# Sparse attention and two mixing layers on one core: GpSimd's two-operand instructions issued in pieces of at most 300 elements

## The chip, the cores and the metric

The kernel runs on one core of a Trainium2 chip. A core has five engines that work side by side, each through its own queue of instructions in order: TensorE (PE in the profile; its weight loads are PEld), VectorE (DVE), ScalarE (ACT), GpSimd (POOL) and SyncE (SP), which here only issues DMAs. They share SBUF, the on-chip memory of 128 partitions; matrix products land in PSUM, which GpSimd doesn't read. The metric is the device time of one execution in microseconds (us).

## What is computed

The reference has three parts. Attention over 4 batches, 8 heads, 576 positions and 64 columns a head keeps the 32 largest scores of each row; two mixing layers follow, the first with a rotation by an angle, the second with a normalised gate.

```python
scores = scale * np.matmul(q, k.transpose(0, 1, 3, 2))
kth = np.partition(scores, -top_k, axis=-1)[..., -top_k:-top_k + 1]
scores = np.where(scores >= kth, scores, -1000000000.0)
attn = np.exp(scores - np.max(scores, axis=-1, keepdims=True))
attn = attn / (np.sum(attn, axis=-1, keepdims=True) + 1e-09)
...
theta = x @ w_theta
y = w_tok_r @ (x * np.cos(theta)) + w_tok_i @ (x * np.sin(theta))
u = x + y
x = u + np.maximum(u @ w_ch, 0.0)
...
h = np.maximum(x @ w_in, 0.0)
u, v = h[..., :d_ff // 2], h[..., d_ff // 2:]
v_s = w_spatial @ normalised(v) + b_spatial
out = (u * v_s) @ w_out
```

The six weights arrive as float64. Products that need near-float32 accuracy are made of three matrix products on operands that are split into a high and a low part; the low part is the difference of a value and its rounded copy, and such differences are much of what GpSimd does.

## The kernel before

Attention runs over 144 tiles (4 batches, 4 pairs of heads, 9 tiles of 128 query rows), two tiles to a group, so 72 groups. `scores` multiplies a tile's queries with the keys and ScalarE copies the 576 scores of each row to `x` (L433). `topk` works on a group's two tiles on VectorE: L448 and L449 halve the row twice by pairwise maximum and minimum (two instructions on 2x288 elements, two on 2x144, listed as 576 and 288), then MAX8 and MATCH_REPLACE8 take out the 32 largest in four rounds. L465 compares four elements a row to `flags`, and L471 makes the threshold `cf`. `weigh` lets ScalarE compute a sign against the threshold (L480) and the exponential (L481); GpSimd multiplies the two into `sg`, 576 elements a tile (L482). `transpose` turns `sg` on TensorE (L491), ScalarE copies the result to `ptb` (L492), and `values` multiplies by the values (L513). `normalise` divides by the row sum, on GpSimd (L544, L547).

Beside that run the conversion of the weights (`split_weights`, L143 to L194: VectorE assembles float32 from the two words of a double, GpSimd makes the high and low part), the preparation of the next heads (`prep`; GpSimd's difference is L374), and the two mixing layers of the batches that are through attention (`rotate`, `middle`, `last`), a few matrix products after each attention step. The mixing layers go through a wrapper `Urgent` that raises an instruction's priority, so the profile shows all of their elementwise work under L568.

No engine's order is written out by hand. The framework's scheduler orders the instructions by priorities and by its own model of their durations. A change in the number or size of instructions can therefore move others on every engine. The program ends with a second, exact copy of all of this that is taken only if a flag is set; it isn't taken here. GpSimd is reached under two names: `pool`, and `upool`, which is `Urgent` around it.

Of the kernel before, what the change touches and what calls it, by code (L numbers as in the profile page):

```python
# [24 lines left out]
def sparse_attention_then_moe_kernel(  # L25
# [20 lines left out]
    nc = tc.nc  # L46
# [25 lines left out]
    dram = ctx.enter_context(tc.tile_pool(name="dram", bufs=1, space=bass.MemoryType.DRAM))  # L72
    psum = ctx.enter_context(tc.tile_pool(name="psum", bufs=1, space=bass.MemoryType.PSUM))

    act, dve, pool, pe = nc.scalar, nc.vector, nc.gpsimd, nc.tensor

    def f32(ap):
        return ap.bitcast(F32)
# [237 lines left out]
    def run(exact):  # L316
# [242 lines left out]
        class Urgent:  # L559
# [5 lines left out]
            def __getattr__(self, name):  # L565
                def call(*args, **kwargs):
                    with tc.high_priority(offset=URGENT):
                        return getattr(self.engine, name)(*args, **kwargs)  # L568

                return call  # L570

        udve, uact, upool = Urgent(nc.vector), Urgent(nc.scalar), Urgent(nc.gpsimd)

        def copy_pool(out, x):
            upool.tensor_scalar(out, x, 1.0, 0.0, op0=OP.mult, op1=OP.add)
# [447 lines left out]
        advance(1e12)  # L1023

    run(False)
    flagged = nc.values_load(count[0:1, 0:1], min_val=0, max_val=128)
    with tc.If(flagged > 0):
        run(True)
# [42 lines left out]
```

## Time and profile before

| | before |
|---|---|
| time, median of 3 runs | 993.77 us (988.09 to 994.96) |
| the profiled execution's own time | 986.55 us |
| its span, first to last instruction | 984.8 us |
| TensorE busy | 854.1 us |
| VectorE busy | 837.5 us |
| ScalarE busy | 626.2 us |
| GpSimd busy | 546.2 us, 476 instructions |

Busy time counts an instruction from its recorded start to its end. An instruction on VectorE or GpSimd that has started and is held up inside still counts as busy, so for these two engines the busy time can hold waiting. Idle time is split by what ended it.

### The profile page before, as it was taken

The page shows a single profiled execution, that of the slowest core. Times are in us where ns is not written, and L with a number is a line of the kernel's source. Part 1 is how long each engine was busy: PE and PEld are TensorE (multiplying, and loading weights), DVE is VectorE, ACT ScalarE, POOL GpSimd, SP SyncE. Part 2 cuts the span into 40 slices and gives each one's busy share as a digit, 9 for nine tenths or more (in the row PEclk, how much of TensorE's full clock was granted, in tenths as well). Part 3 has the DMA queues.
Part 4 walks back from the last instruction along what each step waited for, and adds up shares of the span by engine and source line. Part 5 has one row for each costly group of instructions (what it writes and reads, how often), then busy time and mean ns, then how long its engine had stood idle before and what let it go on. Part 6 is the DMA issues. An engine that isn't in the chain of part 4 may idle for free.

```text
span 984.8 us, 17792 instructions
## 1 busy us (share of the span) xinstructions
PE 854.1 (87%) x5802; PEld 785.8 (80%) x5802; DVE 837.5 (85%) x2710; ACT 626.2 (64%) x1298; POOL 546.2 (55%) x476
## 2 busy tenths in 40 slices
PE   3656677785898999898998999799899999999997
PEld 2555666664797988897898998698889998889987
DVE  6999999899999998899999998999999951463552
ACT  5666767678767567777867777577957764350121
POOL 1686776658685854758385656375655553420030
PEclk9865676687899999999999999899999999999999
DMA  7797774647638463544461844352742645341221
GB/s 218 222 333 224 238 220 150 171 139 203 219 105 241 164 167 140 157 150 100 147 162 32 276 152 144 126 161 71 229 138 68 258 155 181 156 181 52 103 86 53
DMA packets 79393, 159.76 MB, mean 162 GB/s; under 512 B 36143, under 2 KB 40239, under 8 KB 71866
## 3 DMA queue, kind: packets, MB, share of 16 engines
q1 hardware_dynamic: 79290, 158.53, 51.0%
q8 instruction: 48, 0.79, 0.3%
q14 instruction: 55, 0.45, 0.1%
HBM read 108.63 MB, written 23.32 MB: 134 GB/s over the span
## 4 chain that ended last, share of the span: by engine, by line
DVE 46%; PE 32%; ACT 7%; DMA 7%; issue 4%; POOL 3%; SPq 1%; DVEq 0%; ACTq 0%; POOLq 0%
DVE mm L449 8%; PE ps_m L552 7%; DVE mx L458 7%; PE ps_m L553 7%; PE ps_m L554 7%; DVE mm L461 7%; DVE z L452 5%; DVE mm L448 4%; PE ps_v L513 4%; PE ps_s L429 2%; PE ps_t L491 2%; DVE F L568 2%; DMA q<-hi 2%; DVE z L448 2%; DVE cf L471 2%
## 5 line engine op out<-in xcount | busy, mean ns | idle before, releaser
L482 POOL TENSOR_TENSOR sg<-x,sg 128x576 f32<-128x576 f32 x144 | 213.0, 1495 | 150.9 <-ACT x L481 90.9
L513 PE MATMUL ps_v<-vc,ptb 128*128 128x65 f32 (+1 forms) x1280 | 176.6, 277 | 15.1 <-ACT ptb L492 15.1
L513 PEld LDWEIGHTS ps_v<-vc,ptb 128*128 128x128 f32 (+1 forms) x1280 | 167.4, 201 | 24.4 <-ACT ptb L492 18.5
L491 PE MATMUL ps_t<-ident,sg 128*128 128x128 f32 x648 | 132.0, 305 | 42.2 <-POOL sg L482 33.5
L480 ACT ACTIVATE sg<-x,cf 128x576 f32<-128x576 f32 x144 | 103.8, 769 | 56.0 <-DVE cf L471 53.2
L491 PEld LDWEIGHTS ps_t<-ident,sg 128*128 128x128 f32 x648 | 93.7, 166 | 53.9 <-POOL sg L482 39.0
L458 DVE MAX8 mx<-mm 128x8 f32<-128x160 f32 x432 | 118.9, 313 | 0.0
L433 ACT ACTIVATE x<-ps_s 128x576 f32<-128x576 f32 x144 | 92.4, 642 | 32.0 <-POOL sg L482 16.8
L429 PE MATMUL ps_s<-k,q 128*128 128x288 f32 x256 | 91.2, 367 | 24.1 <-ACT x L433 15.0
L552 PE MATMUL ps_m<-w_t,zah 128*128 128x288 f32 (+2 forms) x272 | 98.7, 363 | 11.3 <-DVE F L568 6.7
L481 ACT ACTIVATE x<-x,cf 128x576 f32<-128x576 f32 x144 | 108.0, 767 | 0.1
L492 ACT ACTIVATE ptb<-ps_t 128x640 f32<-128x640 f32 (+1 forms) x144 | 92.4, 642 | 13.2 <-PE ps_t L491 12.3
L554 PE MATMUL ps_m<-w_t,zal 128*128 128x288 f32 (+2 forms) x272 | 96.6, 355 | 0.6 <-DVE zal L568 0.4
L553 PE MATMUL ps_m<-w_t,zah 128*128 128x288 f32 (+2 forms) x272 | 96.5, 355 | 0.0
L452 DVE MAX8 z<-mm 128x8 f32<-128x312 f32 (+1 forms) x288 | 89.5, 372 | 1.9
L552 PE MATMUL ps_m<-w_t,zbh 128*128 128x288 f32 x288 | 85.9, 301 | 3.2 <-DVE F L568 1.9
L461 DVE MATCH_REPLACE8 mm<-mx,mm 128x160 f32<-128x160 f32 x288 | 87.0, 309 | 0.0
L553 PE MATMUL ps_m<-w_t,zbh 128*128 128x288 f32 x288 | 85.4, 300 | 0.6 <-DMA w_t<-d_spl 0.6
L554 PE MATMUL ps_m<-w_t,zbl 128*128 128x288 f32 x288 | 84.3, 299 | 1.0 <-POOL zbl L568 1.0
L552 PE MATMUL ps_m<-ph,w_t 128*128 128x288 f32 x256 | 76.8, 301 | 8.1 <-DMA w_t<-d_chh 4.3
L429 PEld LDWEIGHTS ps_s<-k,q 128*128 128x128 f32 x256 | 55.8, 218 | 33.1 <-ACT x L433 24.6
L449 DVE TENSOR_TENSOR mm<-x 128x576 f32<-128x576 f32 x72 | 82.2, 1141 | 0.0
(175 smaller groups left out, 2391.4 us busy)
## 6 DMA issues: line engine op xcount, KB each, us to landing
k<-hi SPq DMA_DIRECT2D x60, 144.0 KB, 2.6
kl<-raw SPq DMA_DIRECT2D x60, 144.0 KB, 3.1
vc<-in_v_dram SPq DMA_DIRECT2D x48, 128.0 KB, 2.8
w_t<-d_trh SPq DMA_DIRECT2D x4, 1152.0 KB, 5.2
w_t<-d_trl SPq DMA_DIRECT2D x4, 1152.0 KB
out_dram<-t SPq DMA_DIRECT2D x32, 144.0 KB, 2.2
raw<-in_q_dram SPq DMA_DIRECT2D x15, 288.0 KB, 3.0
q<-hi SPq DMA_DIRECT2D x30, 144.0 KB, 2.8
```

The lines of the kernel that those rows point to most:

```text
L429: pe.matmul(o, q, k[:, m], start=a == 0, stop=a == len(terms) - 1)
L449: dve.tensor_tensor(mm[:, :, mid:hi], a, b, op=OP.min)
L452: dve.max(out=z[:, i, QUARTER + 8 * k:QUARTER + 8 * k + 8], in_=mm[:, i, losers])
L458: last = dve.max(out=top[i], in_=src[i])
L461: dve.match_replace(out=mr[i], in_to_replace=top[i], in_values=src[i], imm_value=NEG)
L481: act.activation(x, x, AF.Exp, bias=cf[:, 0:1], scale=0.125)
L482: pool.tensor_tensor(sg, x, sg, op=OP.mult)
L491: pe.transpose(pt[:, c, :], x[:, lo:lo + 128], ident)
L513: pe.matmul(o, pt[:, c, q], chunks[:, c, slot], start=alone and c == 0, stop=not alone and i == 1 and c == 3)
L552: pe.matmul(out, ah, bh, start=first, stop=False)
L553: pe.matmul(out, ah, bl, start=False, stop=False)
L554: pe.matmul(out, al, bh, start=False, stop=last)
```

## The change

The name `pool` no longer stands for GpSimd itself but for an object that passes everything on to it, save `tensor_tensor`: that one is issued in k pieces along the first free dimension, where k is the number of elements a partition divided by 300 and rounded up, but no more than that dimension's length. `upool` is wrapped around the same object. Instructions with one operand (`tensor_scalar`, `memset`) stay whole, and so do those of up to 300 elements.

```diff
-    act, dve, pool, pe = nc.scalar, nc.vector, nc.gpsimd, nc.tensor
+    act, dve, pe = nc.scalar, nc.vector, nc.tensor
+
+    class Pieces:
+
+
+        def __getattr__(self, name):
+            return getattr(nc.gpsimd, name)
+
+        def tensor_tensor(self, out, a, b, op):
+            n = out.shape[1]
+            k = -(-math.prod(out.shape[1:]) // 300)
+            k = min(k, n)
+            cuts = [n * i // k for i in range(k + 1)]
+            for lo, hi in zip(cuts, cuts[1:]):
+                nc.gpsimd.tensor_tensor(out[:, lo:hi], a[:, lo:hi], b[:, lo:hi], op=op)
+
+    pool = Pieces()
...
-        udve, uact, upool = Urgent(nc.vector), Urgent(nc.scalar), Urgent(nc.gpsimd)
+        udve, uact, upool = Urgent(nc.vector), Urgent(nc.scalar), Urgent(pool)
```

All pieces stand under L89 afterwards, and the other lines of the kernel are 16 higher. A shape of three dimensions is cut in its first: the 5x2x64 of `xn` becomes 128, 256 and 256 elements. TensorE's instructions and their order in the last fifth of the program are the same; before that the scheduler has set the order anew.

GpSimd, early in the program, where the first weights are converted (`w_f`, `w_hi`) between multiplications of `sg`. Before:

```order
L194 TENSOR_TENSOR w_f<-w_f,w_hi 128x1024
L374 TENSOR_TENSOR raw<-raw,hi 128x576
L482 TENSOR_TENSOR sg<-x,sg 128x576
L193 TENSOR_SCALAR w_hi<-w_f 128x1152
L482 TENSOR_TENSOR sg<-x,sg 128x576
L194 TENSOR_TENSOR w_f<-w_f,w_hi 128x1152
```

Now, at the same place:

```order
L89 TENSOR_TENSOR w_f<-w_f,w_hi 128x256 x4
L89 TENSOR_TENSOR raw<-raw,hi 128x288 x2
L209 TENSOR_SCALAR w_hi<-w_f 128x1152
L89 TENSOR_TENSOR w_f<-w_f,w_hi 128x288 x4
L89 TENSOR_TENSOR sg<-x,sg 128x288 x6
```

Each whole has become two or four pieces, and the multiplications of `sg` that stood ahead of the 1152-element difference now stand behind its four pieces.

GpSimd in the middle of the program, where `middle` of the first batch splits its `F` (`pl`) beside attention. Before:

```order
L194 TENSOR_TENSOR w_f<-w_f 128x512
L482 TENSOR_TENSOR sg<-x,sg 128x576
L568 TENSOR_TENSOR pl<-F,ph 128x288 x7
L482 TENSOR_TENSOR sg<-x,sg 128x576
L568 TENSOR_TENSOR pl<-F,ph 128x288
L374 TENSOR_TENSOR raw<-raw,hi 128x576
```

Now:

```order
L89 TENSOR_TENSOR w_f<-w_f 128x256 x2
L89 TENSOR_TENSOR pl<-F,ph 128x288 x5
L89 TENSOR_TENSOR sg<-x,sg 128x288 x4
L89 TENSOR_TENSOR pl<-F,ph 128x288
L89 TENSOR_TENSOR raw<-raw,hi 128x288 x2
L89 TENSOR_TENSOR sg<-x,sg 128x288 x2
```

The seven `pl`, which were short enough to stay whole, stood in a row between two `sg`; now five stand ahead of both.

VectorE in the 37th turn of `topk`. Before:

```order
L448 TENSOR_TENSOR mm<-x 128x2x288
L449 TENSOR_TENSOR mm<-x 128x2x288
L465 TENSOR_TENSOR flags<-z,mx 128x4
L471 SCALAR_TENSOR_TENSOR cf<-cf,mx 128x2
L448 TENSOR_TENSOR z<-mm 128x2x144
L449 TENSOR_TENSOR mm<-mm 128x2x144
L452 MAX z<-mm 128x8 x4
```

Now:

```order
L481 TENSOR_TENSOR flags<-z,mx 128x4
L584 TENSOR_TENSOR F<-ps_m,F 128x288 x2
L487 SCALAR_TENSOR_TENSOR cf<-cf,mx 128x2
L464 TENSOR_TENSOR mm<-x 128x2x288
L465 TENSOR_TENSOR mm<-x 128x2x288
L584 TENSOR_TENSOR F<-ps_m,F 128x288
L464 TENSOR_TENSOR z<-mm 128x2x144
L465 TENSOR_TENSOR mm<-mm 128x2x144
L468 MAX z<-mm 128x8 x4
```

The six steps with two operands in SBUF still stand in one stretch; additions to `F` from PSUM, steps of the mixing layers, have moved in between them.

## Rows read from the trace of the kernel before

**Rows 1.** The page: span, and the busiest engines.

```profile
span 984.8 us, 17792 instructions
...
PE 854.1 (87%) x5802; PEld 785.8 (80%) x5802; DVE 837.5 (85%) x2710; ACT 626.2 (64%) x1298; POOL 546.2 (55%) x476
```

**Rows 2.** Busy time by stretch; each engine: us (instructions).

```profile
core 0: us, PE busy (x) PEld busy (x) DVE busy (x) ACT busy (x) POOL busy (x), PEclk, DMA share, GB/s
0.00:200.00 200.00, 130.78 (x627) 111.02 (x628) 187.60 (x589) 133.05 (x263) 125.42 (x116) 0.71 0.74 222
200.00:770.00 570.00, 518.64 (x3755) 483.27 (x3754) 549.99 (x1827) 416.08 (x873) 359.44 (x299) 0.96 0.49 150
770.00:984.00 214.00, 204.64 (x1424) 191.47 (x1423) 99.87 (x296) 77.09 (x162) 61.30 (x61) 0.99 0.38 141
```

**Rows 3.** Groups by line and shape, VectorE: busy us, mean ns, idle before.

```profile
L449 DVE TENSOR_TENSOR mm<-x 128x576 f32<-128x576 f32 x72 | 82.2, 1141 | 0.0
L448 DVE TENSOR_TENSOR mm<-x 128x576 f32<-128x576 f32 x72 | 69.0, 958 | 11.4 <-ACT x L433 11.1
...
L449 DVE TENSOR_TENSOR mm<-mm 128x288 f32<-128x288 f32 x72 | 41.2, 572 | 1.3
...
L448 DVE TENSOR_TENSOR z<-mm 128x288 f32<-128x288 f32 x72 | 35.7, 495 | 0.0
...
L465 DVE TENSOR_TENSOR flags<-z,mx 128x4 uint8<-128x4 f32 x72 | 29.1, 404 | 1.3
L471 DVE SCALAR_TENSOR_TENSOR cf<-cf,mx 128x2 f32<-128x2 f32 x72 | 28.9, 402 | 1.0 <-ACT cf L470 0.6
```

**Rows 4.** Time line of VectorE, an undisturbed turn: start us, us taken.

```profile
166.89 0.16 DVE L465 TENSOR_TENSOR flags<-z,mx 128x4 uint8<-128x4 f32 x1
...
167.57 0.17 DVE L471 SCALAR_TENSOR_TENSOR cf<-cf,mx 128x2 f32<-128x2 f32 x1
167.64 0.46 DVE L448 TENSOR_TENSOR z<-mm 128x288 f32<-128x288 f32 x1
...
169.10 1.24 DVE L452 MAX8 z<-mm 128x8 f32<-128x312 f32 x4
...
174.16 0.75 DVE L448 TENSOR_TENSOR mm<-x 128x576 f32<-128x576 f32 x1
```

**Rows 5.** Time line of GpSimd near 512 us.

```profile
511.94 2.03 POOL L374 TENSOR_TENSOR raw<-raw,hi 128x576 fp32r<-128x576 f32 x1
513.93 1.32 POOL L568 TENSOR_TENSOR pl<-F,ph 128x288 fp32r<-128x288 f32 x1
```

**Rows 6.** Time line of VectorE near 512 us.

```profile
512.60 1.99 DVE L449 TENSOR_TENSOR mm<-x 128x576 f32<-128x576 f32 x1
514.51 0.77 DVE L471 SCALAR_TENSOR_TENSOR cf<-cf,mx 128x2 f32<-128x2 f32 x1
515.20 0.45 DVE L568 TENSOR_TENSOR F<-ps_m,F 128x288 f32<-128x288 f32 x1
```

**Rows 7.** Time line of GpSimd near 328 us.

```profile
327.26 0.79 POOL L568 TENSOR_TENSOR pl<-F,ph 128x288 fp32r<-128x288 f32 x1
328.02 1.41 POOL L374 TENSOR_TENSOR raw<-raw,hi 128x576 fp32r<-128x576 f32 x1
329.40 2.81 POOL L482 TENSOR_TENSOR sg<-x,sg 128x576 f32<-128x576 f32 x2
```

**Rows 8.** Groups by line and shape, GpSimd: largest and smallest with over 300 elements.

```profile
L482 POOL TENSOR_TENSOR sg<-x,sg 128x576 f32<-128x576 f32 x144 | 213.0, 1495 | 150.9 <-ACT x L481 90.9 <-issue 40.2 <-ACT cf L469 13.8
...
L194 POOL TENSOR_TENSOR w_f<-w_f,w_hi 128x576 fp32r<-128x576 f32 x1 | 1.4, 1411 | 0.1
```

**Rows 9.** Who waited for whom: us in total, times, longest.

```profile
PE ps_t L491 <- POOL sg L482: 33.5, 20, 4.6
...
DVE mm L448 <- ACT x L433: 11.1, 10, 3.2
```

**Rows 10.** Time line of GpSimd near 55 us.

```profile
55.26 4.69 POOL L374 TENSOR_TENSOR raw<-raw,hi 128x576 fp32r<-128x576 f32 x1
```

**Rows 11.** Time line of VectorE near 624 us.

```profile
623.95 6.58 DVE L449 TENSOR_TENSOR mm<-x 128x576 f32<-128x576 f32 x1
```

## Prediction: what the pieces do to the time

> **What bounds the kernel now.** I read the totals of the page first. The execution spans 984.8 us, PE is busy 87% of it, DVE 85%, POOL 55% [rows 1]. Such shares average over stages, so the next view was the busy time by stretch [rows 2]. From 0 to 200 us DVE works 187.6 us of 200 and PE 130.8. From 200 to 770 us DVE works 550.0 us of 570 and PE 518.6. From 770 us on it turns round: PE 204.6 us of 214, DVE 99.9. So VectorE sets the pace for the first 770 us and TensorE for the last 214. What shortens VectorE's row of work before 770 us is worth its full length until PE, which has 51 us of idle time between 200 and 770 us, runs out of it.
>
> The next view was VectorE's groups of instructions, with the shapes kept apart [rows 3]. The turn of `topk` for one pair of tiles has six steps with two operands in SBUF: the two of L448/L449 on 576 elements, the two on 288, the flags (L465) and `cf` (L471). There are 72 turns. The means look odd: two instructions of the same shape take 1141 and 958 ns, and the flags, four elements, take 404 ns. A turn in which nothing disturbs shows what they cost by themselves [rows 4]: 0.75 us for 576 elements, 0.46 for 288, 0.16 for the flags, 0.17 for `cf`.
>
> What disturbs them is seen where the two engines' time lines are laid side by side [rows 5, 6]. GpSimd's L374 on 576 elements runs from 511.94 to 513.97 us. VectorE's L449 is listed from 512.60 and takes 1.99 us, which is 1.24 more than its 0.75. Its own 0.75 us would start at 513.84, just before the GpSimd instruction ends. Then GpSimd runs `pl`, 288 elements, from 513.93 to 515.25, and VectorE's `cf` takes 0.77 us, 0.61 too much. It goes the other way too: `pl` takes 1.32 us there, and the same shape takes 0.79 elsewhere [rows 7]. So a VectorE instruction and a GpSimd instruction that both read two operands from SBUF take turns, one whole instruction at a time. Behind a full 576 VectorE loses 1.24 us, behind a full 288 it loses 0.61.
>
> What VectorE loses in this way in the six steps, mean less undisturbed duration, times 72: (1141 - 750) + (958 - 750) + (572 - 460) + (495 - 460) + (404 - 160) + (402 - 170) = 1222 ns, which gives **88 us** [rows 3, 4]. (In the changed kernel's numbering these lines stand 16 higher.)
>
> **The change, part by part.** GpSimd's instructions with two operands and over 300 elements are cut. There are 261 of them in 14 groups of shape and line, from L482 with 213.0 us to the smallest with 1.4 [rows 8]; together they take 395 of POOL's 546 us, 72%. They become 559, so 298 more: 180 from the 180 of 576 elements, 46 from the 46 of 512, 50 from the 25 of 640 (three pieces each), 12 and 6 from the 1152 and 1024, 4 from the 384. Nothing is taken away and no element is computed twice.
>
> *What a piece costs GpSimd.* From start to start, 288 elements take 0.76 us (327.26 to 328.02) and 576 take 1.38 (328.02 to 329.40) [rows 7]. Two pieces cost 2 x 0.76 - 1.38 = 0.14 us more than one whole. Over 298 pieces that is 42 us, and POOL goes from 546 to about 588 us of 985. It stays well under VectorE, so this costs nothing by itself; if the cover is missing it shows up as lateness (below).
>
> *What VectorE gets back.* Three quarters of the 88 us, 66 us, lie behind the cut shapes: they are 72% of POOL's time, and a longer instruction costs more per meeting. How much of the 66 comes back depends on how VectorE's steps stand. Lower bound, nothing: where GpSimd is already busy with a pair of `sg` as the six steps begin, VectorE steps once past each piece instead of once past each whole, and meets four waits of 0.61 instead of two of 1.24. 4 x 0.61 = 2.44 against 2.48. GpSimd's work is the same and VectorE has six steps in a row to spend on it. Upper bound, half: a step that stands alone, with no other two-operand step behind it, waits on the average half a piece where it waited half a whole; 33 us. In between, GpSimd becomes ready while the six steps run, with k of them still to come. With k = 0 to 5 the old wait is 0, 1.24, then 2.48 four times, mean 1.86; the new one is 0, 0.61, 1.22, 1.83, 2.44, 2.44, mean 1.42. That is 24% less. I take one quarter of the 66 us, **17 us**, because the six steps stand close together (undisturbed they add up to 2.75 us), and the MAX8 and MATCH_REPLACE8 steps behind them leave VectorE without a two-operand step for 5 us (169.10 to 174.16) [rows 4], in which GpSimd empties its queue.
>
> *What is late next.* The `sg` of a pair ends later by the four pieces' overhead, 0.28 us, and by up to two more VectorE steps that slip in between. TensorE waits for `sg` 33.5 us in all, 20 times [rows 9]. PE's idle time is not the bound before 770 us, and VectorE itself waits little for what comes round from there: 11.1 us for `x` [rows 9]. I charge 2 us, with 0 and 20 as ends (20 waits by 0.28 + 0.75 us, all of it passed on).
>
> *What the scheduler moves.* The amounts of work and PE's order in the last stretch are unchanged; before it the order differs locally. Near turn 37 two `F` additions now stand between the flags and `cf`. They read PSUM, one such took 0.45 us right behind a wait [rows 6], and GpSimd can run most of a 0.61 us piece under each. At another place three multiplies of `sg` stand behind four `w_f` pieces where two stood ahead of the whole. I count these as zero, with 5 us either way.
>
> *The sum.* The profiled execution took 986.55 us, 1.75 more than its span. 986.55 - 17 + 2 = 971.5 us. The median of the runs of before is 993.77, 7.2 above that execution; on that scale the forecast is **979 us**.
>
> **The rivals.**
> *Half comes back.* The waits are mostly isolated, the 33 us come back and nothing is late: 986.55 - 33 + 7.2 = 961 us. For it: waits behind the long early `w_f` instructions, which are cut in four, and flags steps of four elements that lose 0.24 us on average. Against it: the six steps stand together [rows 4]. The Trainium skill, "SBUF — State Buffer", section "Who interferes with whom", says that VectorE and GpSimd share a port pair under an exclusive lock that is held for the whole instruction, so that the loser blocks fully. The trace agrees in kind (1.24 and 0.61 us), and by the rule read alone, half the hold is half the wait, which is this rival's time.
> *Nothing comes back.* The pieces are all paid one by one, the lower bound: 986.55 + 2 + 7.2 - 2 = 994 us. A harsher form is that VectorE doesn't get in between pieces that follow each other at once. For that there is one row: at 623.95 us L449 took 6.58 us, behind five GpSimd instructions in a row [rows 11]. Against it is that right behind L374 VectorE did get in, and `pl`, which was waiting, paid for it [rows 5, 6].
> *Slower: GpSimd becomes late.* Every piece has to get past VectorE again. At 55.26 us an L374 that takes 1.41 by itself took 4.69, shut out over several VectorE steps [rows 10, 7]. If `sg` comes 1.03 us later at each of the 20 places where PE waits for it, and the loop of scores, `x` and `topk` passes it on, that is 20 us against perhaps 8 gained: 986.55 + 12 + 7.2 = 1006 us. It decides from the point where VectorE's idle time from 200 to 770 us, now 20 us, grows by more than the 17 us saved.
>
> **How the numbers follow.** The forecast (5 to 28 us gained) has 0.50, half 0.15, nothing 0.22, GpSimd late 0.13. About 1%, 10 us, is what a measurement of this kernel can tell from no change. Faster by more than that is the whole of the second case and nearly three quarters of the first: 0.15 + 0.36 = 0.51. Slower is GpSimd late and little else, 0.13. The rest, 0.36, is no change. The likeliest case alone covers 966 to 989 us. The range reaches up past "nothing" to 999 and down past "half" to 957; it leaves out most of the slower case and a tail below.
>
> **What would show it.** L449 and L448 on 576 elements should fall from 1141 and 958 to about 1000 and 900 ns, the flags and `cf` from 404 and 402 to about 330; the six groups' loss should be about 71 us, not 88. Single waits of VectorE of 1.2 us behind GpSimd should be gone, those of 0.6 more frequent. POOL should be busy near 590 us, more if the pieces wait often. VectorE's idle time before 770 us should stay near 20 us and the last stretch should keep its length. Wrong would be: the loss of the six groups unchanged or up (nothing comes back), or the loss down and the idle time of VectorE up by as much (GpSimd late), or a loss under 60 us (half).

## The result, and the profile after

The changed kernel takes **998.23 us** (median of 20 runs, 990.87 to 1004.36). The kernel before, run beside it, takes 990.93 us (20 runs, 985.73 to 996.57). The ratio is **1.0059, 95% interval [1.0042, 1.0076]**: 0.6% slower, within the 1% that the prediction called no change, where 979 us and a gain were forecast. (The ratios here and below are not the quotients of two medians; that quotient is 1.0074 here, and in every run the two agree within 0.2%.) One execution of the kernel before, beside e1 to e4, took 2064.58 us, in a slow state, and is left out of the ratios.

The page of the changed kernel, span and busy time [rows 1 of before]:

```profile
span 996.6 us, 18072 instructions
...
PE 874.2 (88%) x5802; PEld 802.1 (80%) x5802; DVE 822.2 (82%) x2710; ACT 625.6 (63%) x1298; POOL 613.1 (62%) x774
```

VectorE is busy 15.3 us less than in [rows 1], nearly the 17 us that were forecast, and the kernel is longer all the same. GpSimd has the 298 more instructions and is busy 67 us more, not 42. The busy time by stretch [rows 2] shows where the difference went:

```profile
0.00:200.00 200.00, 140.09 (x617) 117.25 (x617) 186.25 (x574) 130.08 (x257) 144.59 (x188) 0.68 0.71 216
200.00:770.00 570.00, 517.82 (x3670) 481.44 (x3671) 531.38 (x1813) 412.44 (x867) 396.71 (x494) 0.96 0.50 152
770.00:996.00 226.00, 216.33 (x1518) 203.44 (x1516) 104.54 (x326) 83.10 (x176) 71.85 (x93) 1.00 0.36 133
```

From 200 to 770 us VectorE works 18.6 us less than in [rows 2], in the same 570 us. It doesn't get further by that: it issues 1813 instructions there, not 1827, and stands idle for 38.6 us, not 20.0. In the first 200 us it issues 574, not 589. TensorE's last stretch is 12 us longer, with 94 more matmuls in it.

VectorE's six steps of `topk` by line and shape, which stand 16 lines higher than in [rows 3]:

```profile
L465 DVE TENSOR_TENSOR mm<-x 128x576 f32<-128x576 f32 x72 | 72.8, 1011 | 0.0
L464 DVE TENSOR_TENSOR mm<-x 128x576 f32<-128x576 f32 x72 | 68.9, 957 | 16.0 <-ACT x L449 15.3 <-ACT cf L486 0.5
L465 DVE TENSOR_TENSOR mm<-mm 128x288 f32<-128x288 f32 x72 | 44.0, 612 | 1.2
L464 DVE TENSOR_TENSOR z<-mm 128x288 f32<-128x288 f32 x72 | 38.3, 531 | 0.0
L481 DVE TENSOR_TENSOR flags<-z,mx 128x4 uint8<-128x4 f32 x72 | 28.0, 389 | 1.3
L487 DVE SCALAR_TENSOR_TENSOR cf<-cf,mx 128x2 f32<-128x2 f32 x72 | 24.3, 337 | 1.9 <-ACT cf L486 1.7
```

By the same working as in the prediction they now lose (261 + 207 + 152 + 71 + 229 + 167) ns x 72 = 78 us to the alternation with GpSimd, 10 less than before. The 576 of L465 (1141 to 1011 ns) and `cf` (402 to 337) gained; the 576 of L464 is where it was, and the two on 288 got worse (572 to 612, 495 to 531).

For all that follows it helps to divide a run at the last turn of `topk` (the last flags instruction). Ahead of it VectorE sets the pace, behind it TensorE does. The row of the changed kernel from 20 us to that point, then the row behind it; the fields are those of [rows 2]:

```profile
20.00:800.90 780.90, 680.43 (x4509) 622.40 (x4509) 735.90 (x2461) 555.16 (x1152) 556.33 (x672) 0.88 0.54 167
800.90:996.60 195.70, 185.88 (x1272) 173.85 (x1270) 74.66 (x202) 60.45 (x128) 53.31 (x68) 1.00 0.36 132
```

And the same two rows of the kernel before:

```profile
20.00:797.30 777.30, 668.42 (x4574) 614.51 (x4575) 752.28 (x2465) 558.27 (x1157) 497.84 (x397) 0.90 0.55 171
797.30:984.80 187.50, 177.72 (x1206) 165.37 (x1204) 73.74 (x199) 58.13 (x123) 44.95 (x46) 0.99 0.33 122
```

Up to the last turn VectorE is busy 16.4 us less (752.28 to 735.90) and idle 20.0 us more (777.30 - 752.28 = 25.0, to 45.0). Behind it, 66 more matmuls take 8.2 us more. Sum: 3.6 + 8.2 = 11.8 us, the difference of the spans. (The profiled execution of before lies 7 us under the median of the runs that the prediction was given, that of after at its own median; the medians of the runs side by side differ by 7.3 us, so some 4 of the 11.8 are the chance of one execution. Which part of it is quick is seen further down, where two more kernels run before's order.)

What VectorE waits for in the loop, in the changed kernel (us in total, times, longest):

```profile
DVE mm L464 <- ACT x L449: 13.1, 13, 2.3
DVE F L584 <- PE ps_m L570: 6.0, 2, 5.5
DVE rs L558 <- ACT xr L538: 4.2, 2, 2.7
DVE zbl L584 <- ACT zbl L584: 3.5, 2, 2.8
DVE F L584 <- PE ps_m L911: 2.8, 3, 1.4
```

and in the kernel before:

```profile
DVE mm L448 <- ACT x L433: 8.9, 9, 3.2
...
DVE F L568 <- PE ps_m L554: 0.7, 1, 0.7
DVE F L568 <- PE ps_m L895: 0.6, 2, 0.5
```

Two kinds of wait grew most: for `x`, which ScalarE makes, and for TensorE's sums that VectorE adds to `F` (1.3 to 8.8 us). The second kind points to the *order*: an addition may now stand ahead of work that could have run while its matmuls finished. So there were two suspects. The theory: the pieces give time, as forecast, and the order that the scheduler made because of them takes it. The rival: the order is nothing, and the pieces themselves cost, by making `sg` late.

### The profile page after: what moved, and what is told of

It is laid out like the page before. It is cut to its first block, busy times and chain, and to the rows that moved or that the text cites. A ratio compares the mean times of both kernels' runs of the same rounds, so it can differ in the third digit from the quotient of the medians.

```text
span 996.6 us, 18072 instructions
## 1 busy us (share of the span) xinstructions
PE 874.2 (88%) x5802; PEld 802.1 (80%) x5802; DVE 822.2 (82%) x2710; ACT 625.6 (63%) x1298; POOL 613.1 (62%) x774
## 4 chain that ended last, share of the span: by engine, by line
PE 43%; DVE 29%; DMA 13%; ACT 7%; POOL 4%; issue 3%; SPq 2%; DVEq 0%; ACTq 0%; POOLq 0%
PE ps_m L570 9%; PE ps_m L568 9%; PE ps_m L569 9%; PE ps_v L529 6%; DVE mx L474 5%; DVE mm L477 5%; DVE mm L465 4%; PE ps_t L507 4%; PE ps_s L445 3%; DVE z L468 3%; DMA q<-hi 3%; DVE mm L464 3%; DMA raw<-in_k_dram 2%; DMA raw<-in_q_dram 2%; DMA k<-hi 2%
## 5 line engine op out<-in xcount | busy, mean ns | idle before, releaser
L89 POOL TENSOR_TENSOR sg<-x,sg 128x288 f32<-128x288 f32 x288 | 239.5, 860 | 123.2 <-ACT x L497 68.1
L529 PE MATMUL ps_v<-vc,ptb 128*128 128x65 f32 (+1 forms) x1280 | 189.9, 288 | 12.3 <-ACT ptb L508 12.3
L529 PEld LDWEIGHTS ps_v<-vc,ptb 128*128 128x128 f32 (+1 forms) x1280 | 180.0, 211 | 23.1 <-ACT ptb L508 16.2
L507 PE MATMUL ps_t<-ident,sg 128*128 128x128 f32 x648 | 139.8, 314 | 35.8 <-POOL sg L89 26.2
L507 PEld LDWEIGHTS ps_t<-ident,sg 128*128 128x128 f32 x648 | 97.4, 172 | 51.0 <-POOL sg L89 35.1
L445 PE MATMUL ps_s<-k,q 128*128 128x288 f32 x256 | 93.8, 377 | 22.8 <-ACT x L449 11.8
L449 ACT ACTIVATE x<-ps_s 128x576 f32<-128x576 f32 x144 | 92.2, 640 | 22.8 <-PE ps_s L445 17.4
L568 PE MATMUL ps_m<-w_t,zah 128*128 128x288 f32 (+2 forms) x272 | 96.9, 356 | 7.3 <-DVE F L584 3.8
L569 PE MATMUL ps_m<-w_t,zah 128*128 128x288 f32 (+2 forms) x272 | 95.5, 351 | 0.0
L445 PE MATMUL ps_s<-kl,q 128*128 128x288 f32 x256 | 83.5, 336 | 0.0
L464 DVE TENSOR_TENSOR mm<-x 128x576 f32<-128x576 f32 x72 | 68.9, 957 | 16.0 <-ACT x L449 15.3
L445 PEld LDWEIGHTS ps_s<-k,q 128*128 128x128 f32 x256 | 58.0, 227 | 29.4 <-ACT x L449 20.5
```

The costliest lines, as they stand in the source:

```text
L89: nc.gpsimd.tensor_tensor(out[:, lo:hi], a[:, lo:hi], b[:, lo:hi], op=op)
L445: pe.matmul(o, q, k[:, m], start=a == 0, stop=a == len(terms) - 1)
L507: pe.transpose(pt[:, c, :], x[:, lo:lo + 128], ident)
L529: pe.matmul(o, pt[:, c, q], chunks[:, c, slot], start=alone and c == 0, stop=not alone and i == 1 and c == 3)
L568: pe.matmul(out, ah, bh, start=first, stop=False)
L569: pe.matmul(out, ah, bl, start=False, stop=False)
```

## The experiments

### Pieces and order taken apart

Every engine's order can be held to a given one: after the program has been traced, each instruction is made to follow the one ahead of it in a recorded list, and the scheduler has nothing left to choose. The pieces of one instruction count as one place. In this way whole instructions run in the changed kernel's order (e1) and pieces run in before's order (e2). The edit that all the held kernels share:

```
+    def held_to(counts, packed):
...
+        for e, n in counts.items():
+            order, steps = np.cumsum(steps[:n]), steps[n:]
...
+            line = [i for k in order for i in units[e][k]]
+            for a, b in zip(line, line[1:]):
+                tc.add_manual_dep(b, a.name, info, reason="held")
...
     run(False)
+    held_to(COUNTS, HELD)
```

e1 is the kernel before with this and the changed kernel's order in HELD; e2 is the changed kernel with this and before's order. In the traces, engine by engine, e1's order is that of the changed kernel and e2's that of the kernel before.

> GpSimd's instructions are whole, as before, but every engine issues its instructions in exactly the order of the changed kernel (the order is written out and held). Theory 'the order costs': the scheduler's new order alone is what made the kernel slower, so this run is slower than before by 1 to 2.5% (1000 to 1015 us beside 990), slower than the changed kernel itself, since the pieces would give some of it back. Rival 'the pieces cost': the new order is as good as the old one, this run is within 0.3% of before.

> GpSimd's instructions are cut into pieces of at most 300 elements, as in the changed kernel, but every engine keeps exactly the order of the kernel before. Theory 'the order costs': the pieces give back what the prediction said, about 15 us, 1 to 2% faster than before (970 to 980 us). Rival 'the pieces cost': slower than before by 0.3 to 1.2%, with VectorE's idle time up and its waits for GpSimd not much smaller in sum.

e1 took 1005.58 us, ratio **1.0117 [1.0084, 1.0150]**, e2 989.89 us, ratio **0.9967 [0.9948, 0.9986]** (before in these runs: 993.77). The new order alone costs 11.6 us. The pieces alone give 3.3 us in before's order, and 5.8 us in the new one (1.0117 to 1.0059). So the sign of the result is the order's. For e2 both accounts missed: the pieces gain, but a quarter of what the theory asked.

Both kernels' rows from 20 us to the last turn, e1 first, e2 in the second fence:

```profile
20.00:808.80 788.80, 680.06 (x4506) 622.96 (x4507) 750.12 (x2462) 555.74 (x1152) 491.93 (x392) 0.89 0.54 165
808.80:1004.60 195.80, 186.43 (x1274) 174.20 (x1273) 76.50 (x203) 60.59 (x128) 49.09 (x52) 0.99 0.36 133
```

```profile
20.00:800.80 780.80, 680.04 (x4575) 621.64 (x4576) 742.24 (x2465) 557.21 (x1157) 560.62 (x677) 0.88 0.55 170
800.80:988.20 187.40, 177.53 (x1206) 165.35 (x1204) 72.03 (x199) 58.39 (x124) 49.53 (x63) 1.00 0.33 122
```

e1 has VectorE's busy time of before (750.12 against 752.28), 13.7 us more idle time, and the longer last stretch (195.8). e2 has 10.0 us less busy time, the last stretch of before (187.4), and again 13.6 us more idle time. Set beside before's quick execution, both idle times look larger than they are. The changed kernel beside e1, pieces beside wholes in the same order, has 14.2 us less busy time and 6.3 more idle time: the pieces bring idle time of their own. ScalarE's wait to write `x` until GpSimd has read the buffer for `sg` grew from 16.8 us in the kernel before to this in e2:

```profile
ACT x L516 <- POOL sg L155: 32.4, 21, 5.6
```

### sg and all the others

In before's order, only the 144 `sg` cut (e3), or all the cut shapes but `sg` (e4):

```
e3:
+        weighing = False
...
+            k = k if pool.weighing else 1
...
+            pool.weighing = True
             pool.tensor_tensor(sg, x, sg, op=OP.mult)
+            pool.weighing = False
e4, in place of the second line:
+            k = k if not pool.weighing else 1
```

> The order of before is held, and only the 144 multiplications of sg are cut in two; the conversions, differences and divisions stay whole. Theory 'the order costs': faster than before by 0.3 to 1%, about half of the gain of cutting all, since sg is 54% of the GpSimd time that is cut. Rival 'the pieces cost': sg is what TensorE waits for, so cutting it makes it later: slower by 0.2 to 1%.

> The order of before is held, and everything but the multiplications of sg is cut: weight conversions (up to 1152 elements), the differences and the divisions. Theory 'the order costs': faster than before by 0.5 to 1.2%, since the longest holds (1024 and 1152 elements, up to 2.4 us a wait) go. Rival 'the pieces cost': within 0.3% of before if the cost is in sg, slower by 0.3 to 0.8% if it is in the first 300 us, where the conversions are.

e3 took 992.38 us, ratio 0.9984 [0.9959, 1.0010]; e4 983.59 us, ratio **0.9903 [0.9870, 0.9936]**. Cutting `sg`, 54% of what was cut by busy time (213 of 395 us), gives nothing that can be told from zero by itself, and takes 6.4 us away when the rest is cut too (0.9903 to 0.9967). e4 is faster than both kernels, by 10 us than before and 15 us than the change. e3 bears out neither account, e4 the theory's. Up to the last turn e4 has the busy time of e2, in the same order, and 4.9 us less idle time (33.7 against 38.6): cutting `sg` on top takes nothing more off VectorE's work and makes it wait.

```profile
20.00:795.50 775.50, 675.56 (x4573) 621.48 (x4574) 741.85 (x2464) 557.84 (x1157) 536.35 (x535) 0.89 0.55 172
```

In e4 ScalarE's wait for `sg` is back near that of before:

```profile
ACT x L519 <- POOL sg L158: 20.2, 15, 2.9
```

### Is it this order, or any other?

Three more orders that the scheduler makes. e5: wholes, held to the order made for pieces of at most 200. e6: all but `sg` cut, as in e4, but scheduled freely. e7: the kernel before with one of the scheduler's numbers moved, which has nothing to do with GpSimd:

```
e6:
-            pool.tensor_tensor(sg, x, sg, op=OP.mult)
+            nc.gpsimd.tensor_tensor(sg, x, sg, op=OP.mult)
e7:
-    FIRST_QUOTA, QUOTA = 2500, 2000
+    FIRST_QUOTA, QUOTA = 2500, 2050
```

> Wholes as before, every engine held to the order that the scheduler makes when it is given pieces of at most 200 elements: a second order made for a cut GpSimd, with 3481 places of TensorE and 1102 of VectorE other than before. If any order that the scheduler makes for a cut GpSimd is bad for the chip, it stands near the first one: 1002 to 1010 us, ratio 1.008 to 1.016. If orders differ by chance around before's, by a per cent or so each, it may fall on either side: 984 to 1004. If order is nothing and the first one was a special accident: 992 to 996.

> All GpSimd instructions cut but the 144 that make sg, in the order that the scheduler makes for that. Held to before's order the same instructions took 983.6 us. If the scheduler's new order costs what it cost the whole change (1.2 per cent): 993 to 998, ratio 1.000 to 1.004. If the order is harmless when sg is whole, because it is sg's longer estimate that moves it: 981 to 987, ratio 0.987 to 0.993.

> Before, with nothing cut, and one number of the scheduler changed (QUOTA 2000 to 2050), which moves 3124 places of TensorE and 879 of VectorE. If the order of before is a lucky one among many that differ by a per cent, a reorder that has nothing to do with GpSimd costs too: 998 to 1010, ratio 1.004 to 1.016. If only orders made for a cut GpSimd cost: 990 to 997, ratio 0.997 to 1.003.

e5 took 1019.74 us, ratio 1.0272 [1.0230, 1.0313]; e6 1012.80 us, 1.0190 [1.0149, 1.0230]; e7 1010.61 us, 1.0187 [1.0153, 1.0220]. All three are slower than anything that was expected of them: a new order costs 2 to 3%, more than the 1.2% of the first one, whether or not it was made for pieces. The same pieces that give 10 us in before's order (e4) lose 19 us in the order that is made for them (e6): the price of that order is some 2.9% (0.9903 to 1.0190).

How an order costs differs. e7 up to the last turn:

```profile
20.00:822.30 802.30, 686.63 (x4568) 629.30 (x4569) 771.38 (x2466) 558.58 (x1157) 500.66 (x399) 0.88 0.54 167
```

VectorE is *busy* 19.1 us more than before with the same instructions: there it loses more to GpSimd (the six steps sum to 307.0 us, 286.1 in [rows 3]; the flags take 522 ns, 404 there). e1 lost its time in idle waits and a longer last stretch instead, and e6 mostly to a last stretch of 201.2 us. At the 56th turn e7 is no later than before (635.2 and 637.5 us); all of its loss comes behind that.

### Where in the program the order costs

Wholes again, with the two orders joined: before's order up to the 26th of the 72 turns and the changed kernel's for the rest (e9), the reverse (e10), and the changed kernel's order up to the 60th turn and before's for the rest (e14). Only the list in HELD differs from e1.

> Wholes; before's order up to the 26th topk turn (some 320 us), and from there the changed kernel's order for what is left. The changed kernel's order from beginning to end cost 1.17 per cent, 11.6 us. If its loss lies in the first 320 us, where turn 25 stood 12 us late in the changed kernel: 991 to 996, ratio 0.998 to 1.003. If it is spread over the whole program, some in every stage: 997 to 1001, ratio 1.004 to 1.008. If it lies behind 320 us: 1002 to 1007.

> The mirror of the run before: wholes, the changed kernel's order up to the 26th topk turn, and before's from there. Loss in the first 320 us: 1002 to 1007, ratio 1.009 to 1.014. Spread: 997 to 1002, ratio 1.004 to 1.009. Loss behind 320 us: 991 to 996.

> Wholes, the changed kernel's order up to the 60th of 72 topk turns, and before's order from there. The changed kernel's order leaves 60 TensorE instructions more behind the last topk turn, and the stretch behind that turn is 195.8 us long instead of 187.4. If the two halves of the order's cost are separate, those 60 come back into the gaps of the loop: the last stretch 187 to 188 us, time 995 to 999, ratio 1.002 to 1.006. If the loop has no room for them and gets longer by as much: 1003 to 1007, ratio 1.010 to 1.014, with the last stretch at 187 all the same.

e9 took 998.67 us, ratio 1.0058 [1.0036, 1.0081]; e10 1002.11 us, 1.0100 [1.0072, 1.0129]; e14 1005.97 us, 1.0136 [1.0107, 1.0165]. By the medians each joined kernel is slower than before, e10 by 8.9 us and e9 by 5.4. e9 is what "spread" asked for; e10 lies at the edge between "spread" and "first 320 us". How much of the new order's loss lies on which side they don't say, since a joint costs too: the 26th, the 29th and the last turn of `topk` end at 312.6, 341.9 and 797.3 us in the kernel before, at 320.9, 358.7 and 813.2 in e10. Half of e10's delay comes in the three turns behind the joint, where e1, with the same order up to there, loses 2.5 us (319.0 and 350.8). Behind the last turn, e9 and e10:

```profile
800.60:997.30 196.70, 186.79 (x1275) 174.27 (x1273) 76.32 (x203) 60.60 (x128) 49.08 (x52) 1.00 0.36 132
```

```profile
813.20:1000.40 187.20, 177.69 (x1206) 165.35 (x1204) 73.78 (x198) 58.07 (x123) 44.98 (x46) 0.99 0.33 122
```

e9 loses in the last stretch, which has 69 more matmuls than e10's. e14 asked whether those can simply go back:

```profile
20.00:821.30 801.30, 690.63 (x4575) 632.75 (x4576) 754.33 (x2466) 558.91 (x1157) 494.95 (x397) 0.91 0.54 166
689.10:821.30 132.20, 126.05 (x939) 119.71 (x939) 119.33 (x408) 93.89 (x188) 73.31 (x60) 0.97 0.47 160
821.30:1009.20 187.90, 177.88 (x1205) 165.32 (x1204) 73.76 (x198) 58.02 (x123) 45.00 (x46) 0.99 0.33 122
```

They can't, as the second account expected. The last stretch is 187.9 us again, but the last turn comes at 821.3 us where e1 had it at 808.8. At the 60th turn e14 is 2 us behind e1 (689.1 and 687.1 us); from there to the last turn it takes 132.2 us where e1 takes 121.7, with 68 more matmuls and TensorE busy 126.1 us of it. (e14's profiled execution is 5 us above its median, so a part of this can be chance.) The matmuls behind e1's last turn are the backlog of an order that had fallen behind: from 20 us to the 60th turn it had issued 3637 matmuls, before's order 3694.

**How much of the idle time is before's quick execution.** Up to the 26th turn e9 runs the instructions of before in the order of before, and so does e7, whose order differs only from some 340 us on. The kernel before, e7 and e9 from 20 us to the end of that turn:

```profile
20.00:312.60 292.60, 216.94 (x1230) 189.75 (x1231) 287.72 (x887) 208.38 (x419) 204.06 (x159) 0.76 0.67 204
20.00:314.90 294.90, 219.55 (x1230) 193.06 (x1231) 287.12 (x886) 208.71 (x419) 202.35 (x159) 0.75 0.66 202
20.00:316.90 296.90, 219.47 (x1220) 193.01 (x1220) 286.39 (x886) 209.48 (x420) 206.76 (x159) 0.74 0.66 200
```

The same program in the same order ends the turn at 312.6, 314.9 and 316.9 us, and VectorE is idle for 4.9, 7.8 and 10.5 us of it. So 3 to 6 us of every increase in idle time that is taken against before's trace can be chance. No run holds the whole of before to its own order, so what holding itself costs isn't measured; up to here no more can be seen than the 2 to 4 us between e9, which is held, and the two others, and e2 to e4 are held and not slower than before.

### Do the pieces and the order add up?

The pieces of e4 in the changed kernel's order (e12; HELD of e1 in e4):

> All GpSimd instructions cut but sg, held to the changed kernel's order. In before's order these cuts gave 1.0 per cent. If the gain of the cuts and the cost of the order add up: 1.0117 less 0.010, 993 to 998, ratio 1.000 to 1.005. If the cuts give what they give only in an order whose waits leave room for it, or the new order's waits eat it: 1000 to 1008, ratio 1.007 to 1.015.

e12 took 1000.88 us, ratio 1.0094 [1.0067, 1.0121]. As the second account had it, they don't add up: in this order the same cuts give 2.3 us (1.0117 to 1.0094) where they gave 9.6 in before's, and cutting `sg` as well gives 3.5 more (to 1.0059) where it took 6.4 away. The 2.3 us are within the noise of the two runs and the 3.5 barely beyond it; that the cuts give less here than in before's order is clear of it. What a piece is worth depends on what stands around it.

### Is it sg's lateness?

Wholes in before's order, with one more GpSimd instruction of one element a partition ahead of each `sg`; it reads `x`, so it starts when `sg` could have. It has one operand in e11 and two in e13.

```
e11:
-            pool.tensor_tensor(sg, x, sg, op=OP.mult)
+            a = pool.tensor_scalar(late[:, n % 32:n % 32 + 1], x[:, 0:1], 1.0, 0.0, op0=OP.mult, op1=OP.add).ins.name
+            PIECES.append([a, pool.tensor_tensor(sg, x, sg, op=OP.mult).ins.name])
e13, in place of the first of these two:
+            a = pool.tensor_tensor(late[:, n % 32:n % 32 + 1], x[:, 0:1], x[:, 1:2], op=OP.mult).ins.name
```

> Wholes in before's order, and ahead of each of the 144 instructions that make sg one more GpSimd instruction of one element a partition that reads the same x, so that it waits for the same thing: it makes sg later by some 0.2 to 0.3 us, about as much as two pieces do, and GpSimd busier by some 35 us, without any more handovers between the engines. If sg's lateness by itself is what cutting sg costs: 4 to 9 us more, 997 to 1003, ratio 1.004 to 1.009, with longer waits of ScalarE for sg before it copies x. If the lateness is covered, as the 2 us of the prediction said, and it is the handovers that cost: 992 to 996, ratio 0.998 to 1.003.

> As the kernel with one more GpSimd instruction of one element ahead of each sg, but that instruction has two operands instead of one. In the kernel with the one-operand instruction, VectorE stood four times behind 4 to 7 GpSimd instructions without a gap (17.0 us in all, 5.8 us in the kernel before), each time from a request that fell into a one-operand instruction. If those long refusals are what made that kernel 8 us slower, and a one-operand instruction brings them on: at most two waits behind 3 or more instructions, 992 to 996. If it is the lateness of sg itself, whatever instruction makes it late: 998 to 1004 again.

e11 took 1000.50 us, ratio 1.0080 [1.0049, 1.0111]; e13 999.46 us, 1.0080 [1.0051, 1.0109]. The added instruction takes about 0.19 us (durations: least, median, longest, in ns; e11):

```profile
L548 POOL TENSOR_SCALAR late<-x x144: 182/193/2126, 22.8 to 817.6; 128x1 f32<-128x1 f32 x144
```

With some 0.2 us more ahead of each `sg`, and nothing cut and nothing reordered, the kernel is 8 us slower. In e11 VectorE stood four times behind 4 to 7 GpSimd instructions in a row (17.0 us; before has one such wait, of 5.8 us), so e11 alone couldn't tell lateness from these waits. e13 has two of them, 9.7 us, and is as slow. Its row to the last turn, then to the 29th turn, and e7's to the 29th turn, the end of before's order in e7:

```profile
20.00:809.60 789.60, 675.87 (x4573) 622.09 (x4574) 754.63 (x2464) 557.21 (x1157) 514.93 (x539) 0.88 0.55 168
20.00:353.60 333.60, 249.02 (x1405) 221.64 (x1406) 317.80 (x983) 227.02 (x458) 230.87 (x236) 0.74 0.65 196
20.00:345.30 325.30, 245.17 (x1410) 217.85 (x1410) 317.25 (x983) 227.55 (x458) 225.91 (x180) 0.76 0.65 201
```

At the 29th turn e13 is 8.3 us behind e7, 7.7 of them VectorE's idle time (15.8 against 8.1); behind that turn hardly anything is added (e13 is 11.7 us behind before there, 12.3 at the last turn). So the delay costs, and it costs in the first 350 us. It delays whatever stands behind `sg` on GpSimd as well, which these two runs don't separate. Nor do they show the path: ScalarE's wait for `sg` before it writes `x`, which the first account of e11 expected to grow, is 19.5 us in e11 and 18.9 in e13, where before has 16.8 and e9 18.5; and from 20 us to the 29th turn VectorE doesn't wait for `x` in any of them. What is longer there in e13 than in e7 are its waits for `cf` (4.0 us against 0.9) and for the weights' buffer `w_f` (4.3 against 2.8).

### Shorter still

e4 with pieces of at most 150 elements, in before's order (e8):

```
-            k = -(-math.prod(out.shape[1:]) // 300)
+            k = -(-math.prod(out.shape[1:]) // 150)
```

> All GpSimd instructions but sg cut to at most 150 elements (a 576 in four, a 1152 in eight), in before's order. At most 300 gave 983.6 us. If a shorter hold is what pays, and VectorE waits for the end of the running piece: 978 to 982, VectorE's busy time down by another 3 to 8 us. If the pieces' overhead of 0.14 us each and the more frequent alternations take it back: 984 to 992, with as many more VectorE instructions that wait, each for less.

e8 took 1010.99 us, ratio 1.0174 [1.0141, 1.0208]: 27 us slower than e4, a miss for both accounts. The overhead is there (330 more pieces, GpSimd busy 62.8 us more, 0.19 us a piece with its waits for VectorE), but the trace has something else too. GpSimd near 272 us (start, us taken):

```profile
271.31 2.78 POOL L158 TENSOR_TENSOR sg<-x,sg 128x576 f32<-128x576 f32 x2
274.05 1.84 POOL L158 TENSOR_TENSOR w_f<-w_f 128x144 fp32r<-128x144 f32 x4
275.84 1.82 POOL L158 TENSOR_TENSOR raw<-raw,hi 128x144 fp32r<-128x144 f32 x4
277.62 1.82 POOL L158 TENSOR_TENSOR w_f<-w_f 128x144 fp32r<-128x144 f32 x4
```

and VectorE at the same time:

```profile
272.59 6.87 DVE L551 TENSOR_TENSOR flags<-z,mx 128x4 uint8<-128x4 f32 x1
279.39 0.68 DVE L656 SCALAR_TENSOR_TENSOR angle<-t,ps_m 128x512 f32<-128x512 f32 x1
```

A flags instruction of four elements is listed with 6.87 us, stands behind 14 GpSimd instructions without a gap, and comes in as the last of them ends (279.44). e8 has six waits behind three or more, 26.1 us together; e4 has one, 3.3 us. Cutting a whole doesn't open a door at every cut. How much of the 27 us is these waits and how much the later `sg` (ScalarE's wait to write `x` is 43.6 us here, 20.2 in e4) can't be told from this run.

All kernels, with the division at the last turn (us; busy and idle time of VectorE from 20 us on):

| kernel | order | ratio | busy | idle | last stretch |
|---|---|---|---|---|---|
| before | before's | 1 | 752.3 | 25.0 | 187.5 |
| after | changed | 1.0059 | 735.9 | 45.0 | 195.7 |
| e1 wholes | changed | 1.0117 | 750.1 | 38.7 | 195.8 |
| e2 pieces | before's | 0.9967 | 742.2 | 38.6 | 187.4 |
| e3 only `sg` cut | before's | 0.9984 | 746.7 | 34.8 | 188.0 |
| e4 all but `sg` cut | before's | 0.9903 | 741.9 | 33.7 | 187.4 |
| e6 the same | its own | 1.0190 | 747.1 | 37.3 | 201.2 |
| e12 the same | changed | 1.0094 | 741.5 | 40.6 | 196.4 |
| e8 the same, 150 | before's | 1.0174 | 752.2 | 52.6 | 189.4 |
| e5 wholes | for 200 | 1.0272 | 771.8 | 42.5 | 182.6 |
| e7 wholes | quota 2050 | 1.0187 | 771.4 | 30.9 | 184.8 |
| e9 wholes | before's, then changed | 1.0058 | 741.7 | 38.9 | 196.7 |
| e10 wholes | changed, then before's | 1.0100 | 753.6 | 39.7 | 187.2 |
| e14 wholes | changed, before's from turn 60 | 1.0136 | 754.3 | 47.0 | 187.9 |
| e11 late `sg` | before's | 1.0080 | 759.7 | 33.1 | 187.4 |
| e13 late `sg` | before's | 1.0080 | 754.6 | 35.0 | 187.7 |

The last three columns come from one execution each, and before's is a quick one (986.55 us, where the runs of it that are compared lie between 985.73 and 999.71); the ratios come from several.

TensorE's clock is a rival that the experiments above leave open, and the executions' own figures close it for the main steps. Over an execution the granted clock is on average 0.909 in the kernel before (56 executions), 0.909 in e1, 0.908 in e2, 0.911 in e11, 0.910 in e13 and 0.906 in the changed kernel. Among the 56, one hundredth less goes with some 3.6 us more; which is the cause isn't shown. An estimate by that slope: the clock of the changed kernel goes with 1 of its 7 us, the lower clocks of e5 to e8 (0.896 to 0.904) go with 2 to 5 of their 17 to 27 us, and e4's 0.916 with 2 of its 10.

## Why the prediction was wrong

**The number.** 998.23 us lie just inside the stated range (957 to 999), and that is luck: the range was put around a gain and around "nothing comes back" at 994, and neither is what happened. Two terms missed by some 10 us each, the order and the pieces' net gain.

**What bounds the kernel** was right: VectorE up to the last turn, TensorE behind it, and all the kernels' times divide along that line.

**What VectorE loses and gets back.** The alternation is there as read, and VectorE's busy time fell by about what was forecast: 11.8 us from before to e2, 15.7 from e1 to after (page totals 837.5 to 825.7, 837.9 to 822.2), for 17. But only 7 to 9 us of it are in the six steps (286.1 to 277.6 us and 283.4 to 276.3, summed over the six rows), half of what the model of k ready instructions gave; the rest is in VectorE's other work, and that the total comes near 17 is partly luck. An order alone moves the six steps by more, with wholes: to 275.3 us in e9, to 307.0 in e7. The 576 of L449 (now L465) came to 1011 ns where 1000 was forecast, that of L448 to 957 for 900, the flags and `cf` to 389 and 337 for 330. The pieces' overhead on GpSimd was under-sized too, 67 us of busy time for 42, since pieces also wait for VectorE.

**The step that failed first: the order, counted as zero with 5 us either way.** It costs 11.6 us (e1, 1.17% of 993.77 us), more than any other term. The prediction had seen two places where it differs and judged them by what GpSimd could do under them. What it missed is that the order of before is not one among equals: each of the three other orders that the scheduler made costs 1.2 to 2.7% with wholes (e1, e5, e7), in different ways: idle waits, more time lost to GpSimd, a backlog behind the last turn. "The last stretch should keep its length" was wrong for the same reason.

**The step that failed second: the price of a later `sg`, 2 us with ends 0 and 20.** Some 0.2 us ahead of each `sg` cost 8 us (e11, e13), inside the two ends but four times the term. The sum charged a lateness that is covered where PE waits; but in the first 350 us what is late on GpSimd comes round to VectorE as idle time (7.7 us at the 29th turn of e13), by a path that isn't shown. So VectorE's busy time is in part traded for its own idle time: from e1 to the changed kernel 14.2 us less busy and 6.3 more idle, and from e4 to e2 no less busy and 4.9 more idle. The pieces' net term was forecast at 15 us and is 3.3 (before's order) to 5.8 us (the new order).

**The rivals.** "GpSimd becomes late" named the point from which it would decide: VectorE's idle time from 200 to 770 us up by more than 17 us. It rose by 18.6, and the kernel became slower, 7 us instead of the 12 of its price. But the lateness is only part of that idle time: some of it is before's quick execution, and e1 has 13.7 us more, up to the last turn, with no piece at all. "Nothing comes back" in its harsher form, VectorE not getting in between pieces, had one row [rows 11]; e8 shows that it is a mechanism. Its milder form named 994 us, nearest to the measured time, but for a reason that failed: VectorE did get busy time back. Half came back nowhere. The rule of the Trainium skill, "SBUF — State Buffer", section "Who interferes with whom", by which the loser blocks for the whole instruction, agrees with most waits: of the 2782 over 0.1 us in the sixteen traces 2590 were behind one GpSimd instruction. What the rival drew from it, that half the hold is half the wait, fails: a quarter of the hold gave the longest wait of all (e8, 6.87 us with its own 0.15).

**What stays open.** Why before's order is so much better than its neighbours isn't shown, only that it is, and that either half of the new order costs something. By which path a later GpSimd makes VectorE idle isn't shown; more than three buffers of `x` were not tried.

## What to carry to other kernels

Where a scheduler orders the program by estimated durations, a change of durations is two changes: hold the old order and time the parts one by one, because a new order of a tuned kernel cost 1 to 3% here, more than the pieces gave in any order. With `sg` whole and before's order held, the same idea gave 1.0% instead of losing 0.6%, though in the changed kernel's order `sg` was no worse cut than whole. And count an engine's saved busy time as a gain only after the engine's idle time has been looked at in the same stretch.

## What the runs showed of the hardware

- A GpSimd instruction of a single element takes 0.19 us, with one operand (median 193 ns of 144, e11) or with two (196 ns, e13). A cut costs 0.14 us, in e8 as in [rows 7]: four pieces of 144 take 1.79 us from start to start (274.05 to 275.84), a whole of 576 takes 1.38. GpSimd's busy time grew by more, 0.19 us a piece from e4 to e8 and 0.22 in the changed kernel, since it holds waits for VectorE.
- A wait is here a two-input instruction of VectorE that is listed over 0.1 us longer than the shortest of its shape. All 2782 of the sixteen traces began while GpSimd ran an instruction; in 352 of them that one had one operand. Such instructions hold VectorE off as well, which the prediction's alternation left out: 309 of the 318 waits behind a single one of them ended within 0.25 us of its end.
- VectorE doesn't always get in when a GpSimd instruction ends. 23 of these waits were behind 3 to 14 GpSimd instructions that followed each other without a gap, for up to 6.7 us; 16 of the 23 began in an instruction with one operand. What decides it isn't shown.
- The longest such row is 14 instructions in e8, 5 in the kernel before, 4 in the changed one, and 7 in e11 and e13, where nothing is cut.
